# Attention and a gated mixture of experts on one core: a hand-searched order of TensorE's steps, and one weight load moved

## The chip, the cores and the metric

One core of one Trainium2 chip runs the whole kernel. The metric is the device time of one execution in microseconds (us), as the median of several runs. The core's engines work side by side, each through its own list of instructions: TensorE (PE) multiplies, its weight loads are shown apart as PEld; VectorE (DVE), ScalarE (ACT) and GpSimd (POOL) work elementwise; SyncE (SP) and GpSimd issue transfers. Semaphores make one engine wait for another.

## The reference

Sliding-window attention with four "sink" keys, for 4 batches, 8 heads, 768 positions and 64 elements a head, and then a mixture of 4 experts over the 3072 rows of 512 that come out of it:

```python
keep = is_sink | in_window                       # 4 sinks, a window of 128
scores = np.where(keep, q @ k.T / sqrt(D), -1e9)
a = exp(scores - max) / sum
x = (a @ v)  -> rows of H * D = 512

p = domain_probs / domain_probs.sum(-1)
for e in range(4):
    h = np.maximum(x @ w1[e], 0.0)               # 512 -> 1024
    out += p[:, e:e + 1] * (h @ w2[e])           # 1024 -> 512
```

## The kernel before

**Tiles and stages.** The work is cut by batch b (0 to 3) and by group g of 256 rows (three to a batch). Attention of a group runs by head pairs hp (four): `scores` (L676, products over 64 rows of the array, one half of it for each head of the pair), an exponential on ScalarE (L702), a mask on VectorE (L695), `values` (L743, and L736 for the sink part), a reciprocal and a scaling into `onat`. Sink scores are a product of their own (`sinks`, L637). In batch 0 q and k are transposed on TensorE (`transposes`, called "flip", L570) and the result rows too (`turn`, L801); from batch 1 on both go by transposing DMAs on SyncE's queue (L245 into `qkT`, L760 into `xT`).

The mixture takes a group's `xT` through expert e. A unit is one (b, g, e). A slow unit makes x @ w1 in four steps (L1051); a fast one uses a Strassen form of seven products P1 to P7 (L1138) on sums of tokens (`T`, VectorE) and of weights. The relu of batch 0 has no gate and may run on ScalarE or VectorE ("any"; L1064 and L1066 for slow units, L1157 and L1159 for fast ones). From batch 1 on it is fused with the gate on VectorE. The second product is `second` for batch 0 (L1388, 512 columns) and, from batch 1 on, `product`, a Strassen chain over all four experts (L1312, 256 columns) in the order P1, P2, P6, P5, P7, P3, P4. Six H buffers hold units between the two products. Six PSUM banks turn round among the attention's and the first products' tiles; two more hold the second products' sums.

**What sets the order.** There is no fixed list. The kernel, while it is being built, keeps a clock for each engine in the table `t` and emits instructions as it goes. The main loop (from L1446) runs until nothing is left. In each round it first issues transfers that are due from the list `loads` and transposes from `turns`, then work of the other engines up to TensorE's planned time (`flush`), token sums (`mix.tokens`) and sums for the Strassen forms (`mix.chore`, `next_form`). Then it lists TensorE's options, each with a planned ready time and a rank: attention steps (rank `DUE` when attention lags, else 3; a double score block 0.1 lower), `product` (`LOW_PRODUCT`, or -1 when VectorE is behind by more than `BEHIND` or `FULL` units live), steps of open units (2 + `STEP0` x position), opening a new unit (`OPEN`, less `EARLY` for a batch from 1 on), and `second` (1 or `LOW_SECOND`). It takes the one that is ready within 40 ns and has the lowest rank, or, where none is, the one ready first (L1512). About 700 such choices are made.

A score block is emitted for one head pair ("todo") or for two ("two"), where four PSUM banks are free at once.

**The other engines.** `later(engine, ready, slack, run)` puts an item on the list `pend`; `flush` (L145) serves the engine whose next start is earliest, and on it the item with the earliest ready + slack. An item marked "any" goes to ScalarE or VectorE, whichever is served first. The slacks are constants: `MASK_SLACK` for the masks of batches 1 to 3, `TOKEN` for token sums, `GATE` for gated relus, `FORM` for weight sums. `MARGIN` enters the due times of the sums of H.

**Loads.** `load_nat`, `load_v`, `load_w1` and `load_w2` issue on GpSimd's queue in the order of `loads`; for a batch's rows (q, k) a block is two transfers of 128 KB, v is one, a w1 or w2 is 1024 KB. When batch 0's attention is through (L1452), the loop adds w1 of expert 3, then for each row block tb of batch 1 its q and k, with v behind every second block; w2 of expert 3 stands ahead of block tb = `LAST`, 2. `turn_nat` plans when a block's transpose is through, with `LATE` added. `values_at` holds when a group's values are planned to be through.

**Batches.** The attention of batch b + 1 starts when batch b's is through and the mixture's work has passed a share `LEAD` of what lies ahead of it.

The choice itself is one line, L1512:

```python
        r, _, kind, step = min(opts, key=lambda o: (o[0] > now + 40, o[0] if o[0] > now + 40 else 0, o[1]))
```

Of the kernel before, what the change touches and what calls it, by code (L numbers as in the profile page):

```python
# [16 lines left out]
def kernel(  # L17
# [28 lines left out]
    NHP = H // 2  # L46
# [19 lines left out]
    LOW_PRODUCT = 2.147  # L66
    LOW_SECOND = 2.509
    HIGH_PRODUCT = -1
    EARLY = 0.1973
    MASK_SLACK = 200.0  # L70
    GATE = 2639.0
    GATE0 = 6000.0
    FORM = 1000.0
    TOKEN = 4559.0
    MARGIN = 2117.0
    HOLD = 0
    FULL = 8
    STEP0 = 0.2923
    READY = 40
    WIDE = 3  # L80
    OPEN = 2.551
    ONACT = 1
    ONE = 2
    PAIR = 0
    BEHIND = 2351.0
    CHORES = 3
    OWN = 2
    LAST = 2
    BIASED = 1
    FAST = tuple(START)  # L90
    BZ = 0
# [32 lines left out]
    def free_at(n=1):  # L124

        return sorted(ring)[n - 1]
# [276 lines left out]
    def next_form():  # L403

        if forming:
            return False
        x = next(((weight_form1, e) for e in FAST if form1_due(e)), None) or next(
            ((weight_form, e) for e in range(E) if form_due(e)), None)
        if x is None:
            return False  # L410

        def run(engine):
            forming.clear()
            x[0](x[1])
        forming.append(x)
        later("dve", t["pe"], FORM, run)
        return True

    forms_at = {}
# [237 lines left out]
    def scores(b, hp, g, more=False):  # L657
# [32 lines left out]
        if b == 0:  # L690
            part = join(2, masked)
        else:
            def mask_both(at):
                def run(engine):
                    nc.vector.tensor_mul(a, a, m[:, None, :].to_broadcast([P, 2, w]))  # L695
                    masked(dve(2 * w, rate=1.92))

                later("dve", at, MASK_SLACK, run)
            part = join(2, mask_both)
        for ph in range(2):  # L700
            def run(engine, ph=ph):
# [18 lines left out]
    def values(b, hp, g):  # L720
# [96 lines left out]
    class Attention:  # L817
# [15 lines left out]
        def more(self):  # L833
            return bool(self.todo or self.scored or self.valued)

        def two(self):
            return self.b >= PAIR and len(self.scored) <= 2 and len(self.todo) > 1 and self.todo[0][::3] == self.todo[1][::3] and self.todo[0][0] == "scores"

        def flip_ready(self):
            _, b, g, hp = self.flips[0]  # L840
# [3 lines left out]
        def options(self):  # L844

            if self.valued:
                yield turn_ready(*self.valued[0]), "turn"
            if self.scored and len(self.valued) < 3:
                yield values_ready(*self.scored[0]), "values"
            if self.todo:  # L850
                kind, b, x, y = self.todo[0]
                if kind == "scores":
                    if len(self.scored) < 4:
# [64 lines left out]
    class Mixture:  # L918
# [77 lines left out]
        def firsts(self):  # L996

            early = sum(map(len, self.early.values()))
            zero = sum(u["unit"][0] == 0 for u in self.open)
            n = len(self.open)  # L1000
            for i, u in enumerate(self.open):
                b, g, e = u["unit"]
                if u["fast"]:
                    for m in u["left"]:
                        yield max(u["at"].get(m, 1e12), free_at() if m == "P5" else 0.0), 2 + STEP0 * i, (u, m)
                else:
                    j = u["left"][0]
                    yield self.unit_ready(b, g, e, j < QF // 2), 2 + STEP0 * i, (u, j)
            if n < WIDE and early:
                at, g = self.next_early()  # L1010
                yield at, (OPEN if n else 2), ("early", g)
            if n < WIDE and self.units and early <= MIX and self.room() and not (early + zero and self.live >= NH - 1):
                yield self.unit_ready(*self.units[0], False), (OPEN if n else 2) - EARLY, ("unit",)

        def emit_first(self, what, ready):

# [57 lines left out]
            def run(engine):  # L1074
# [3 lines left out]
                at = dve(2 * G, fixed=152)  # L1078
                take(slot, at)
                part(at)  # L1080
            later("dve", end, GATE0, run)

        def tokens(self):

# [8 lines left out]
            if at > t["pe"]:  # L1093
                return
            at = t["pe"]
            x = xT[b, g]
# [9 lines left out]
            def run(engine):  # L1106
# [6 lines left out]
            later("dve", at, TOKEN, run)  # L1113

        def emit_fast(self, u, m, ready):
            b, g, e = u["unit"]
# [61 lines left out]
                later("dve", ready, slack, run)  # L1178

            if m == "P1":  # L1180
                u["last"] = join(2, lambda at: gated(H[:, 1, :, 1], tiles["X"], 1, at, GATE, slots["X"]))

                def seed(engine):
                    nc.scalar.copy(out=tiles["Y"], in_=y)  # L1184
# [15 lines left out]
            elif m == "P6":  # L1200
                u["both"](end)
            elif m == "P2":
                gated(H[:, 0, :, 1], y, 1, end, GATE, slots["Y"])
            elif m == "P7":
                def run(engine):
                    nc.vector.tensor_add(c5, c5, y)  # L1206
                    at["P4"] = dve(n)
                    gated(H[:, 1, :, 0], c5, 0, at["P4"], 100, then=u["last"])
                later("dve", end, 0, run)
            elif m == "P3":  # L1210
                gated(H[:, 0, :, 0], y, 0, end, GATE, slots["V"])
            else:
                u["last"](end)

        def chore(self):

            if self.chores >= CHORES:
                return False

            def go(fn, slack):  # L1220
# [43 lines left out]

        def until(self, b, g, e, m):
            n = self.products.index((b, g, m)) * E + self.order_of(b, g).index(e) - self.piece
            return max(0.0, n * QF * G / 2.4 - MARGIN)

        def operand(self, b, g, e, m):
            H = self.H[b, g, e]  # L1270
# [170 lines left out]
    def free_ring(x):  # L1441
        if ahead < 1 or turns and x[1] <= turns[0][0]:
            return True
        return t["hw"] < t["pe"] and not (turns and (turns[0][0], 0) in turned_at)

    while mix.more() or att.more():  # L1446
# [43 lines left out]
        due = ahead == 0 or att.steps * share <= (mix.done - upto) * att.total  # L1490
        opts = []
        if att.more():
            opts = [(max(r, now), (DUE if due else 3) - 0.1 * (step == "two"), "att", step) for r, step in att.options()]
        s2, p = mix.second_ready(), mix.product_ready()
        behind = max(t["dve"] - now, 0.0) + 500 * sum(x[2] == "dve" and x[0] < now + 300 for x in pend)
        opts.append((max(p, now), HIGH_PRODUCT if behind > BEHIND or mix.live >= FULL else LOW_PRODUCT, "product", None))
        opts += [(max(f, now), p, "first", x) for f, p, x in mix.firsts()]
        opts.append((max(s2, now), 1 if mix.since >= 1 else LOW_SECOND, "second", None))
# [6 lines left out]
        if soonest > 1e11:  # L1505
# [52 lines left out]
```

## Time and profile before

| | us |
|---|---|
| median of 3 runs | 363.13 |
| lowest, highest | 362.83, 363.67 |
| the profiled execution | 362.99 |
| its span | 361.2 |
| PE busy | 351.7 |
| DVE busy | 296.4 |
| ACT busy | 164.9 |
| POOL busy | 70.4 |

The span runs from the first instruction to the last; the profiled execution's time has 1.8 us more around it. Busy times are of one profiled execution. Matmuls overlap, so that a row's "mean ns of one" is a latency; the pace is read from the difference of two starts. A few matmul records are missing from a trace, so that a group of eight may be shown with seven. "Releaser" or "<-" names what ended an idle time. A line number is that of the kernel before.

### The profile page before, as it was taken

The page shows a single profiled execution, that of the slowest core. Times are in us where ns is not written, and L with a number is a line of the kernel's source. Part 1 is how long each engine was busy: PE and PEld are TensorE (multiplying, and loading weights), DVE is VectorE, ACT ScalarE, POOL GpSimd, SP SyncE. Part 2 cuts the span into 40 slices and gives each one's busy share as a digit, 9 for nine tenths or more (in the row PEclk, how much of TensorE's full clock was granted, in tenths as well). Part 3 has the DMA queues.
Part 4 walks back from the last instruction along what each step waited for, and adds up shares of the span by engine and source line. Part 5 has one row for each costly group of instructions (what it writes and reads, how often), then busy time and mean ns, then how long its engine had stood idle before and what let it go on. Part 6 is the DMA issues. An engine that isn't in the chain of part 4 may idle for free.

```text
span 361.2 us, 10566 instructions
## 1 busy us (share of the span) xinstructions
PE 351.7 (97%) x4410; PEld 296.2 (82%) x4423; DVE 296.4 (82%) x671; ACT 164.9 (46%) x419; POOL 70.4 (19%) x90
## 2 busy tenths in 40 slices
PE   8799999998999999999999999999999999999996
PEld 3485767756668868898899899899999999999985
DVE  4665999868868979789789989979999998987840
ACT  5764634557754463655464465546222223212110
POOL 8935016223500616101440000000000000000000
PEclk9999999999999999999999999999999999999999
DMA  9999999999943999917899131214113102000011
GB/s 172 182 186 201 210 209 177 149 126 184 149 92 97 146 175 152 135 49 74 128 155 174 16 104 31 55 50 62 37 25 89 31 22 85 16 29 33 0 61 58
DMA packets 117292, 37.25 MB, mean 103 GB/s; under 512 B 100613, under 2 KB 112741, under 8 KB 117245
## 3 DMA queue, kind: packets, MB, share of 16 engines
q0 software_dynamic: 77520, 17.31, 56.1%
q1 hardware_dynamic: 38668, 18.75, 26.0%
q8 instruction: 34, 0.56, 0.6%
q10 hardware_dynamic: 1056, 0.52, 0.5%
q14 instruction: 14, 0.11, 0.2%
HBM read 40.45 MB, written 6.34 MB: 130 GB/s over the span
## 4 chain that ended last, share of the span: by engine, by line
PE 72%; DMA 21%; POOL 4%; issue 1%; DVE 1%; ACT 0%; SPq 0%
PE acc L1312 31%; PE cps L1138 27%; DMA w<-in_moe_w_dram 11%; PE hps L1051 6%; DMA qkn<-in_k_dram 4%; DMA vx<-in_v_dram 3%; PE acc L1388 3%; DMA xT<-onat 2%; PE sps L676 2%; PE od L743 2%; POOL qkn L233 1%; POOL vx L298 1%; PE od L736 1%; POOL w L311 1%; POOL w L321 0%
## 5 line engine op out<-in xcount | busy, mean ns | idle before, releaser
L1138 PEld LDWEIGHTS <-w 128*128 128x128 bf16 x1184 | 73.3, 98 | 3.7 <-issue 1.5
L1312 PEld LDWEIGHTS <-H 128*128 128x128 bf16 x600 | 56.0, 98 | 6.2 <-issue 0.6
L702 ACT ACTIVATE aT<-sps 128x512 bf16<-128x512 f32 (+1 forms) x96 | 47.4, 573 | 18.5 <-PE sps L676 18.5
L1171 DVE SCALAR_TENSOR_TENSOR H<-cps,gates 128x512 bf16<-128x512 f32 x78 | 52.9, 682 | 1.3 <-PE cps L1138 0.2
L1138 PEld LDWEIGHTS <-vf 128*128 128x128 bf16 x768 | 47.3, 98 | 1.7 <-issue 0.4
L1312 PE MATMUL acc<-w,H 128*128 128x256 bf16 x360 | 47.7, 273 | 0.0
L1138 PE MATMUL cps<-T,w 128*128 128x128 bf16 x592 | 45.1, 219 | 0.1
L1138 PE MATMUL cps<-xT,w 128*128 128x128 bf16 x592 | 44.8, 219 | 0.0
L1388 PE MATMUL acc<-w,H 128*128 128x512 bf16 x179 | 43.4, 379 | 1.0 <-issue 0.5
L782 ACT ACTIVATE onat<-od,R 128x64 bf16<-128x64 f32 x144 | 32.9, 324 | 23.9 <-DVE R L770 23.9
L1051 PE MATMUL hps<-xT,w 128*128 128x256 bf16 x352 | 43.5, 273 | 0.1
L1184 ACT COPY cps<-cps 128x512 f32<-128x512 f32 x37 | 21.4, 579 | 38.4 <-PE cps L1138 32.8
L1138 PE MATMUL cps<-T,vf 128*128 128x128 bf16 x512 | 38.3, 219 | 0.1
L1051 PEld LDWEIGHTS <-w 128*128 128x128 bf16 x352 | 32.9, 98 | 5.6 <-issue 1.3
L1388 PEld LDWEIGHTS <-H 128*128 128x128 bf16 x192 | 17.8, 98 | 17.9 <-issue 0.3
L298 POOL DMA_DIRECT2D vx<-in_v_dram x24 | 21.4, 901 | 48.8 <-PE od L743 44.8
L1312 PEld LDWEIGHTS <-S 128*128 128x128 bf16 x288 | 27.2, 98 | 2.9 <-issue 0.2
L1191 DVE TENSOR_TENSOR cps<-H,cps 128x512 f32<-128x512 f32 x31 | 21.4, 692 | 8.4 <-PE cps L1138 5.5
L1360 ACT COPY osb<-acc 128x256 f32<-128x256 f32 x28 | 10.5, 373 | 38.3 <-PE acc L1312 38.3
L1312 PE MATMUL acc<-wf,H 128*128 128x256 bf16 x184 | 25.8, 273 | 0.0
L695 DVE TENSOR_TENSOR aT<-aT,mask 128x1024 bf16<-128x1024 bf16 (+1 forms) x36 | 22.8, 640 | 1.9 <-ACT aT L702 1.7
L1206 DVE TENSOR_TENSOR H<-H,cps 128x512 f32<-128x512 f32 x31 | 21.2, 683 | 3.8 <-PE cps L1138 3.7
(126 smaller groups left out, 543.9 us busy)
## 6 DMA issues: line engine op xcount, KB each, us to landing
w<-in_moe_w_dram POOLq DMA_DIRECT2D x7, 1024.0 KB, 16.2
out_dram<-osb SPq DMA_DIRECT2D x19, 256.0 KB
gates<-gate_rows SPq DMA_DIRECT2D x36, 128.0 KB
vx<-in_v_dram POOLq DMA_DIRECT2D x24, 128.0 KB, 6.9
qkn<-in_q_dram POOLq DMA_DIRECT2D x22, 128.0 KB, 6.8
qkn<-in_k_dram POOLq DMA_DIRECT2D x22, 128.0 KB, 7.2
w<-in_moe_w_dram POOLq DMA_DIRECT2D x2, 512.0 KB, 9.0
out_dram<-osl SPq DMA_DIRECT2D x4, 256.0 KB
```

What stands on the lines that cost most here:

```text
L298: nc.gpsimd.dma_start(out=vx[tb][:, :, 0:D], in_=v[b, :, tb * P:(tb + 1) * P, :].rearrange("h p d -> p h d"),)
L695: nc.vector.tensor_mul(a, a, m[:, None, :].to_broadcast([P, 2, w]))
L702: nc.scalar.activation(out=a[:, ph], in_=sps[ph][:, 0:w], func=AF.Exp, scale=scale)
L782: nc.scalar.mul(o[:, qi, hp, ph * D:(ph + 1) * D], od[:, qi, ph, 0:D], R[:, qi, ph])
L1051: nc.tensor.matmul(h[:, i].rearrange("p (q n) -> p q n", q=2), lhsT=w1_sb[e][:, db, fb * P:(fb + 1) * P], rhs=xT[b, g][:, :, db], start=(i ...
L1138: nc.tensor.matmul(y[:, f], lhsT=A[:, d, f * P:(f + 1) * P], rhs=T[:, d], start=(m in ("P1", "P5") and f == 0 and d == 0), stop=(d == 1), ...
L1171: nc.vector.scalar_tensor_tensor(out=dst, in0=src, scalar=0.0, in1=gate, op0=ALU.max, op1=ALU.mult)
L1184: nc.scalar.copy(out=tiles["Y"], in_=y)
L1191: nc.vector.tensor_add(tiles["V"], c5, tiles["X"])
L1206: nc.vector.tensor_add(c5, c5, y)
L1312: nc.tensor.matmul(x, lhsT=self.operand(b, g, e, m)[:, f], rhs=forms[e][m][:, f], start=(k == 0 and f == 0 and m in (("P1", "P5", "P2") if ...
L1388: nc.tensor.matmul(op, lhsT=H[:, fb // QF, fb % QF, s], rhs=w2_sb[e][:, fb, :], start=(fb == 0), stop=(fb == NFB - 1),)
```

## The change

The diff turns many of the planner's constants into tuples of four, read by `by(x)`: which entry counts depends on TensorE's planned time against `SPLIT` (60, 130 and 220 us). Most tuples repeat the old value four times. The entries that differ are in the diff below. In words:

- `OTHER` lists 30 of the main loop's choices by number, with 1, 2 or 3: at these the option with that place in the sorted list is taken, not the first (the last one, if the list is shorter).
- An "any" item is open to VectorE only if ScalarE's planned free time is not earlier than VectorE's plus `ANYLAG` (0, and 51.99 ns past 220 us).
- `LAST` 2 becomes 0: w2 of expert 3 is asked for right behind w1 of expert 3, ahead of all of batch 1's rows.
- `LATE` 500 becomes 618.6, `LEAD`'s first entry 1.026 becomes 1.027, and `DUE`, `MASK_SLACK`, `TOKEN`, `MARGIN`, `FULL` and `OPEN` change in some stretches.
- New switches stand at values that leave the old course: `FORCE`, `HELD`, `GPOS`, `LOADN`, `TOKENS0`.
- `values_at` is set at the fourth head pair of a group alone.

```diff
+    HELD = ("unit", "early")
     NGATE = 5
+    ANYLAG = (0.0, 0.0, 0.0, 51.99)
+    OTHER = {31: 1, 83: 1, 70: 1, 73: 1, 63: 3, 17: 1, 138: 1, 106: 1, 189: 1, 92: 1, 113: 2, 149: 2, 87: 1, 182: 2, 96: 3, 178: 2, 132: 1, 90: 1, 155: 1, 164: 1, 318: 1, 286: 2, 330: 1, 197: 1, 395: 1, 212: 2, 480: 1, 454: 2, 569: 2, 500: 2}
+    TOKENS0 = 0.0
+    SPLIT = (60000.0, 130000.0, 220000.0)
...
-    LEAD = (1.026, 0.9853)
-    DUE = 1.356
+    LEAD = (1.027, 0.9853)
+    DUE = (1.356, 1.646, 1.356, 1.356)
...
-    MASK_SLACK = 200.0
+    MASK_SLACK = (200.0, 984.1, 200.0, 200.0)
...
-    TOKEN = 4559.0
-    MARGIN = 2117.0
+    TOKEN = (4927.0, 4559.0, 4924.0, 4559.0)
+    MARGIN = (4621.0, 2117.0, 2117.0, 2117.0)
     HOLD = 0
-    FULL = 8
+    FULL = (8, 8, 8, 9)
...
-    OPEN = 2.551
+    OPEN = (2.551, 2.566, 2.551, 2.551)
...
-    LAST = 2
+    LAST = 0
+    GPOS = 0
+    LOADN = 0
...
+    def by(x):
+
+        return x[sum(t["pe"] > at for at in SPLIT)]
+
...
-    FLIP, LATE = 103.6, 500.0
+    FLIP, LATE = 103.6, 618.6
...
-                mine = [x for x in pend if x[2] == engine or x[2] == "any" and engine != "pool"]
+                mine = [
+                    x for x in pend if x[2] == engine or x[2] == "any" and (
+                        engine == "act" or engine == "dve" and max(t["act"], x[0]) >= max(t["dve"], x[0]) + by(ANYLAG))
+                ]
...
-        values_at[b, g] = done
+        if hp == NHP - 1:
+            values_at[b, g] = done
...
-    loads, turns = [(load_nat, 0, tb) for tb in (4, 5)] + [(load_v, 0, (4, 5))], []
+    loads, turns = [], []
     for e in (1, 2):
         loads += [(load_w1, e), (load_w2, e)]
+    loads[GPOS:GPOS] = [(load_nat, 0, tb) for tb in (4, 5)] + [(load_v, 0, (4, 5))]
...
-        if not att.more() and not loaded:
+        if not loaded and (len(loads) < LOADN if LOADN else not att.more()):
...
-        r, _, kind, step = min(opts, key=lambda o: (o[0] > now + 40, o[0] if o[0] > now + 40 else 0, o[1]))
-        assert r < 1e11
+        opts = [o for o in opts if o[0] < 1e11]
+        opts.sort(key=lambda o: (o[0] > now + 40, o[0] if o[0] > now + 40 else 0, o[1]))
+        r, _, kind, step = opts[min(OTHER.get(taken, 0), len(opts) - 1)]
+        taken += 1
```

More of the change, by code (lines that the diff above doesn't have):

```diff
@@ L415, in next_form @@
         forming.append(x)
-        later("dve", t["pe"], FORM, run)
+        later("dve", t["pe"], by(FORM), run)
         return True
@@ L696, in run @@
                     masked(dve(2 * w, rate=1.92))
-                later("dve", at, MASK_SLACK, run)
+                later("dve", at, by(MASK_SLACK), run)
             part = join(2, mask_both)
@@ L834, in more, with mate @@
             return bool(self.todo or self.scored or self.valued)
+        def mate(self):
+            return self.b >= by(PAIR) and len(self.todo) > 1 and self.todo[0][::3] == self.todo[1][::3] and self.todo[0][0] == "scores"
         def two(self):
-            return self.b >= PAIR and len(self.scored) <= 2 and len(self.todo) > 1 and self.todo[0][::3] == self.todo[1][::3] and self.todo[0][0] == "scores"
+            return len(self.scored) <= 2 and self.mate()
         def flip_ready(self):
@@ L852, in options @@
                 if kind == "scores":
-                    if len(self.scored) < 4:
+                    if len(self.scored) < 4 and not (by(FORCE) and self.mate()):
                         yield scores_ready(b, x, y), "todo"
@@ L1004, in firsts @@
                     for m in u["left"]:
[L1005 removed]
+                        yield max(u["at"].get(m, 1e12), free_at() if m == "P5" else 0.0), 2 + by(STEP0) * i, (u, m)
                 else:
                     j = u["left"][0]
[L1008 to L1009 removed]
+                    yield self.unit_ready(b, g, e, j < QF // 2), 2 + by(STEP0) * i, (u, j)
+            if n < by(WIDE) and early:
                 at, g = self.next_early()
[L1011 to L1013 removed]
+                yield at, (by(OPEN) if n else 2), ("early", g)
+            if n < by(WIDE) and self.units and early <= MIX and self.room() and not (early + zero and self.live >= NH - 1):
+                yield self.unit_ready(*self.units[0], False), (by(OPEN) if n else 2) - by(EARLY), ("unit",)
         def emit_first(self, what, ready):
@@ L1080, in run @@
                 part(at)
-            later("dve", end, GATE0, run)
+            later("dve", end, by(GATE0), run)
         def tokens(self):
@@ L1092, in tokens @@
             at = max(xT_at.get((b, hp, g), 1e12) for hp in range(NHP))
-            if at > t["pe"]:
+            if at > t["pe"] or b == 0 and t["pe"] < TOKENS0:
                 return
@@ L1112, in run @@
                     self.T_at[b, g] = done
-            later("dve", at, TOKEN, run)
+            later("dve", at, by(TOKEN), run)
         def emit_fast(self, u, m, ready):
@@ L1180, in emit_fast @@
             if m == "P1":
-                u["last"] = join(2, lambda at: gated(H[:, 1, :, 1], tiles["X"], 1, at, GATE, slots["X"]))
+                u["last"] = join(2, lambda at: gated(H[:, 1, :, 1], tiles["X"], 1, at, by(GATE), slots["X"]))
                 def seed(engine):
@@ L1202, in emit_fast @@
             elif m == "P2":
-                gated(H[:, 0, :, 1], y, 1, end, GATE, slots["Y"])
+                gated(H[:, 0, :, 1], y, 1, end, by(GATE), slots["Y"])
             elif m == "P7":
@@ L1210, in emit_fast @@
             elif m == "P3":
-                gated(H[:, 0, :, 0], y, 0, end, GATE, slots["V"])
+                gated(H[:, 0, :, 0], y, 0, end, by(GATE), slots["V"])
             else:
@@ L1215, in chore @@
         def chore(self):
-            if self.chores >= CHORES:
+            if self.chores >= by(CHORES):
                 return False
@@ L1266, in until @@
             n = self.products.index((b, g, m)) * E + self.order_of(b, g).index(e) - self.piece
-            return max(0.0, n * QF * G / 2.4 - MARGIN)
+            return max(0.0, n * QF * G / 2.4 - by(MARGIN))
         def operand(self, b, g, e, m):
@@ L1444, in free_ring @@
         return t["hw"] < t["pe"] and not (turns and (turns[0][0], 0) in turned_at)
+    taken = 0
     while mix.more() or att.more():
@@ L1492 @@
         if att.more():
-            opts = [(max(r, now), (DUE if due else 3) - 0.1 * (step == "two"), "att", step) for r, step in att.options()]
+            opts = [(max(r, now), (by(DUE) if due else 3) - 0.1 * (step == "two"), "att", step) for r, step in att.options()]
         s2, p = mix.second_ready(), mix.product_ready()
         behind = max(t["dve"] - now, 0.0) + 500 * sum(x[2] == "dve" and x[0] < now + 300 for x in pend)
-        opts.append((max(p, now), HIGH_PRODUCT if behind > BEHIND or mix.live >= FULL else LOW_PRODUCT, "product", None))
-        opts += [(max(f, now), p, "first", x) for f, p, x in mix.firsts()]
-        opts.append((max(s2, now), 1 if mix.since >= 1 else LOW_SECOND, "second", None))
+        opts.append((max(p, now), HIGH_PRODUCT if behind > by(BEHIND) or mix.live >= by(FULL) else by(LOW_PRODUCT), "product", None))
+        hold = by(FORCE) and due and att.two() and max(turned(att.b, att.todo[0][3], *(att.todo[i][2] for i in range(2)))) < now and free_at(4) > now
+        opts += [(max(f, now), p, "first", x) for f, p, x in mix.firsts() if not (hold and x[0] in HELD)]
+        opts.append((max(s2, now), 1 if mix.since >= 1 else by(LOW_SECOND), "second", None))
         soonest = min(o[0] for o in opts)
```

23 lines of the change are left out of this document (12 added, 11 removed).

## The prediction

> **What bounds the kernel now.** I read the page's busy times first, then the same by stretches, then what TensorE waited for. The page:
>
> ```profile
> span 361.2 us, 10566 instructions
> PE 351.7 (97%) x4410; PEld 296.2 (82%) x4423; DVE 296.4 (82%) x671; ACT 164.9 (46%) x419; POOL 70.4 (19%) x90
> ```
>
> By stretches (from and to in us, length, then busy us of PE, PEld, DVE, ACT and POOL with counts, granted clock, DMA share, GB/s):
>
> ```profile
> 0.00:10.00 10.00, 7.85 (x50) 3.82 (x50) 4.66 (x28) 5.70 (x13) 8.99 (x16) 1.00 1.36 170
> 10.00:20.00 10.00, 8.53 (x122) 5.67 (x121) 7.97 (x29) 8.06 (x18) 8.45 (x14) 1.00 1.68 189
> 40.00:50.00 10.00, 9.95 (x92) 7.44 (x91) 9.69 (x21) 4.27 (x10) 1.75 (x2) 1.00 1.18 210
> 80.00:90.00 10.00, 8.90 (x103) 6.08 (x103) 8.32 (x17) 7.08 (x24) 2.60 (x4) 1.00 1.38 181
> 90.00:100.00 10.00, 9.89 (x113) 6.08 (x114) 8.05 (x18) 7.70 (x26) 5.52 (x7) 1.00 2.20 152
> 120.00:130.00 10.00, 9.16 (x110) 7.01 (x109) 7.95 (x21) 4.58 (x10) 5.04 (x6) 1.00 2.38 153
> 190.00:200.00 10.00, 10.00 (x139) 9.10 (x137) 9.90 (x25) 4.42 (x14) 0.00 (x0) 1.00 1.08 150
> 350.00:361.20 11.20, 8.05 (x74) 6.96 (x72) 1.68 (x5) 1.12 (x3) 0.00 (x0) 1.00 0.13 47
> ```
>
> TensorE is the bound: 9.5 us of the span (361.2 - 351.7) are not busy. Of these 3.6 lie in the first 20 us (20 - 7.85 - 8.53), 3.2 in the tail after its last product (11.2 - 8.05), 1.10 in 80 to 90 and 0.84 in 120 to 130; 0.8 is left for all the rest, and at 190 a busy figure shows nothing to win. The granted clock is whole in each row. The waits of PE, in us in total, times, and the longest:
>
> ```profile
> PE acc L549 <- DVE lent L467: 1.4, 1, 1.4
> PE tr L570 <- DMA qkn<-in_k_dram: 1.1, 1, 1.1
> PE sinks L637 <- DMA qkT<-qkn: 0.8, 1, 0.8
> PE od L743 <- DVE aT L695: 0.7, 1, 0.7
> PE od L743 <- DMA vx<-in_v_dram: 0.6, 1, 0.6
> ```
>
> The first is the start, before any choice. The third and fourth are what a new order can still take away: 0.80 and 0.68 us, here in their places (start, length, instruction, the idle time before it):
>
> ```profile
> 84.32 0.29 PE L637 MATMUL sinks<-qkT,ksd 128*32 128x256 bf16 x4 [0.80 <-DMA qkT<-qkn]
> 129.43 0.35 PE L743 MATMUL od<-vx,aT 128*128 128x65 bf16 x6 [0.68 <-DVE aT L695]
> ```
>
> A busy PE hides one more cost, the crossing into and out of the score blocks, whose products use 64 rows of the array:
>
> ```profile
> 95.17 1.04 PE L1051 MATMUL hps<-xT,w 128*128 128x256 bf16 x8
> 96.14 0.39 PE L676 MATMUL sps<-qkT 64*128 64x128 bf16 x6
> 96.47 1.05 PE L1051 MATMUL hps<-xT,w 128*128 128x256 bf16 x8
> 97.35 1.89 PE L1388 MATMUL acc<-w,H 128*128 128x512 bf16 x7
> ...
> 99.17 0.62 PE L676 MATMUL sps<-qkT 64*128 64x128 bf16 x12
> 99.72 1.05 PE L1051 MATMUL hps<-xT,w 128*128 128x256 bf16 x8
> ```
>
> Read the starts. Eight L1051 products ahead of a score block take 0.97 us (96.14 - 95.17), the same eight ahead of another full-array product 0.88 (97.35 - 96.47): the entry costs 0.09. A lone score block (x6, one head pair) lasts 0.33 to the next start, a double (x12, two head pairs) 0.55. So two lone blocks cost 2 x (0.33 + 0.09) = 0.84, one double 0.55 + 0.09 = 0.64: each merge saves 0.20 us. The timeline has 14 lone blocks in batches 1 to 3, the first and the last being
>
> ```profile
> 73.74 0.34 PE L676 MATMUL sps<-qkT 64*128 64x256 bf16 x4
> ...
> 202.84 0.34 PE L676 MATMUL sps<-qkT 64*128 64x256 bf16 x4
> ```
>
> so at most 7 merges, 1.4 us, are left.
>
> The Trainium skill says that changing the tiling mode drains TensorE (TensorEngine Tiling (Array Packing), Tiling Modes, Key Properties), and TensorE: Matmul & The Clock Gate (Single matmul latency) puts a drain at about 175 ns. By these a merge would save an estimated 0.35 us, two drains, and the three merges of the sum below 1.05 in place of 0.6, for 361.4; the rows' 0.20 for a whole merge is the measurement and decides.
>
> **The change part by part.** Dead parts first. The new condition lets VectorE take an "any" item only if ScalarE's planned free time is at least VectorE's plus a lag. The lag is 0 until the planned TensorE time passes 220 us, and with 0 it says what the old rule says already: an engine is served when its next start is the earliest, ties going to ScalarE. The relus of the first batch, and the two copies of the "any" kind (L269), have ended by then:
>
> ```profile
> L1064 ACT ACTIVATE H<-hps x23: 597/597/636, 19.6 to 126.4; 128x512 bf16<-128x512 f32 x23
> L1157 ACT ACTIVATE H<-cps x13: 592/597/606, 54.8 to 85.2; 128x512 bf16<-128x512 f32 x13
> L269 ACT COPY xT<-tx x5: 367/372/392, 15.0 to 42.0; 128x256 bf16<-128x256 bf16 x5
> ```
>
> The last starts at 126.4, so the placing by backlog comes to 0. That holds unless other edits push a relu past 220 us, which none can. DUE and OPEN in their second phase move a rank between the same neighbours (1.646 stays between 1 and 2, 2.566 between 2.509 and 2.5846); FULL 9 guards a count that six H buffers cap; MARGIN 4621 applies below 60 us, where the sums it dates (chores of batch 1) do not exist yet; FORCE, HELD, LOADN, GPOS and TOKENS0 are off at their values; values_at is read only after the fourth head pair. All 0.
>
> LEAD[0] + 0.001 starts batch 2's attention a thousandth of the work ahead of it later, some 0.1 us of a third of the span, with products in its place: 0. LATE adds 0.12 us to when the planner believes a turned block of batches 1 to 3. It guards against waits like the 0.80 above, and its cost is a score block 0.12 later behind other products: 0 to +0.1, taken 0. TOKEN (4927 and 4924 for 4559) lets the token sums sit 0.37 us lower in VectorE's order, 0. MASK_SLACK (984 for 200) in 60 to 130 us lets VectorE put a mask (L695) up to 0.78 us later. Between a score block and its values lie products (L1051 and L1388 in the rows at 95 to 100), which cover that; the 0.68 above is such a cover run out, and a mask 0.78 later would add up to that much. I take 0 and keep +0.8 for the range.
>
> **The last w2** is asked for ahead of batch 1's first rows. Its neighbours on the POOL queue, and the chain of waits with what landed when (start, length):
>
> ```profile
> 27.83 0.75 POOL L311 DMA_DIRECT2D w<-in_moe_w_dram  x1
> ...
> 50.57 0.87 POOL L321 DMA_DIRECT2D w<-in_moe_w_dram  x1 [4.30 <-DMA w<-in_moe_w_dram]
> ```
> ```profile
> 27.83 27.32 DMA w<-in_moe_w_dram
> 56.34 14.92 DMA qkn<-in_k_dram
> 73.33 12.36 DMA vx<-in_v_dram
> ```
> ```profile
> 57.17 26.84 SPq L245 DMA_TRANSPOSE qkT<-qkn  x6
> ```
>
> The last w1 landed at 55.15 (27.83 + 27.32). Behind it stood two blocks of q and k and two of v, then the 1 MB of w2, then the other four blocks, of which the third's k landed at 71.26. One MB at the 210 GB/s of 40 to 50 us is 5.0 us. So the first two blocks, and batch 1's first scores at 73.74, come up to 5.0 us later: between 73.7, if the planner's wait and the transposing queue (26.84 us for six blocks) have slack, and 78.7. I take the middle. Blocks three to six have the same bytes ahead of them as before: 0, and so the sinks' 0.80 wait gets no worse by this. TensorE has products of the first batch in the meantime (9.95 busy in 40 to 50), and w2 itself lands some 3.7 us sooner (0.75 MB fewer ahead of it), which frees its products that much earlier: 0. If that cover is gone, up to +5.0.
>
> **The thirty listed steps.** Each takes the second, third or fourth of the ready list, so the same products in another order; the sum of PE work stays, and only merges and waits can change. Step 17 can be followed. The loop is the same up to it: values of the fourth head pair go ahead of the fourth pair's transposes.
>
> ```profile
> 12.10 0.49 PE L570 MATMUL tr<-ident,qkn 128*128 128x128 bf16 x3
> 13.73 0.90 PE L570 MATMUL tr<-ident,qkn 128*128 128x128 bf16 x13 [1.15 <-DMA qkn<-in_k_dram]
> ```
>
> PE's wait for the k rows falls after three transposes, inside the first head pair's, ahead of the swap: nothing is won there, at most 0.2 lost or gained in the order behind it. The other 29 act on a state that the earlier ones have changed. I bound them. Best: all 7 merges (1.4) and both waits (1.5) gone, -2.9. Worst: a wait like the 0.80 for each of a few steps, +2.4 for three. Counted along the old order, step 106 is the lone block at 73.74, so a product is to go ahead of it, after which a second head pair may have its banks and the two merge; steps 182 and 197 have lone blocks second on their lists, so they may part a pair as well as shift one. 20 of the 29 lie below step 200, which stood at 130 us: they reach the stretches with 1.10 and 0.84 idle. For the value I take half of the best, as the ends are far apart and the rows show both the idle time and the lone blocks to be there: three merges (0.6) and one of the two waits (0.7), -1.3.
>
> **The sum.** The profiled execution took 362.99 us, 361.2 of it span. 362.99 - 1.3 = 361.7; the median of three lies 0.14 above the profiled execution, so 361.8.
>
> **Rivals.** A, the order does not do what it is listed for: the steps exchange one lone block for another and the waits move, 363.1 (within 0.4). For it: PE's products are fixed and its row at 190 is full. Against: the two waits and 14 lone blocks.
>
> B, more: six merges and most of both waits, -2.5, so 362.99 - 2.5 + 0.14 = 360.6. Against: some head pairs are alone because a PSUM bank was not free.
>
> C, slower, by batch 1's rows: its first scores start past 76 us, the first batch's products run short before its first xT is turned, and PE waits once, between 95 and 130 us, for half of the 5.0: 363.13 + 2.5 = 365.6. It decides from the point where PE's wait for qkT or xT exceeds 1.3, the gain. For it: the w2 is ahead of what the next attention needs. Against: PE at 9.95 of 10 in 40 to 50 and 9.89 in 90 to 100, with products at hand on both sides.
>
> D, VectorE: masks or gated products late in 60 to 210 us, where DVE is at 9.90 of 10, so PE waits for aT or H two or three times at 0.7, less the merges: 363.13 + 1.6 - 0.6 = 364.1.
>
> **How the numbers follow.** Forecast 0.40, A 0.23, B 0.15, C 0.12, D 0.10. A measurement here tells 0.2%, 0.7 us, from no change. The forecast's own range is 361.0 to 362.6; most of it and all of B are faster by over 0.2%, a piece of A too: 0.54. The rest of A and the forecast's upper end are the same: 0.24. C and D: 0.22. The range reaches to B and through D, and cuts the upper half of C: 360.2 to 364.6.
>
> **What would show it.** Right: under 12 lone score blocks in batches 1 to 3, the idle before the first sinks or the value block under 0.3, PE's busy total lower by the merges, the tail still about 3.2. The w2 right: batch 1's first scores between 74 and 79, with no idle of PE before them. Wrong: 14 lone blocks and the same waits (A); an idle of PE over 1.3 us between 95 and 130 on qkT, xT or w (C); several on DVE (D). A relu of the first batch on another engine than before, at an unchanged place in the order, would show that the placing is not dead.

## The result, and the profile after

| | before | after |
|---|---|---|
| median, us (16 runs each) | 362.66 | 360.64 |
| ratio, 95% interval | | 0.9953 (0.9938 to 0.9968) |
| the profiled execution, us | 362.99 | 361.27 |
| its span, us | 361.2 | 359.6 |

The change makes the kernel 0.47% faster, about 1.7 us by the ratio, which is that of the means; the medians differ by 2.0. The page after, first two lines:

```profile
span 359.6 us, 10578 instructions
PE 351.3 (98%) x4424; PEld 296.5 (82%) x4424; DVE 297.1 (83%) x673; ACT 163.7 (46%) x417; POOL 70.4 (20%) x90
```

TensorE still bounds it, with 8.3 us of its span idle (359.6 - 351.3). What PE waited for (us in total, times, longest):

```profile
PE sps L691 <- DMA qkT<-qkn: 1.9, 1, 1.9
PE acc L564 <- DVE lent L482: 1.4, 1, 1.4
PE tr L585 <- DMA qkn<-in_k_dram: 1.2, 1, 1.2
PE od L758 <- DMA vx<-in_v_dram: 0.3, 2, 0.2
PE tx L817 <- DVE onat L788: 0.2, 1, 0.2
```

Against the same view of before, the waits of 0.8 (sinks for qkT) and 0.7 (values for a mask) are gone, and a new one of 1.9 has come, the largest in the kernel. The stretches show the same (from and to, length, busy us of PE, PEld, DVE, ACT and POOL, clock, DMA share, GB/s):

```profile
0.00:10.00 10.00, 8.26 (x52) 4.01 (x54) 4.86 (x28) 5.84 (x13) 8.99 (x16) 1.00 1.33 169
10.00:20.00 10.00, 8.44 (x122) 5.59 (x122) 7.92 (x29) 7.91 (x18) 8.47 (x14) 1.00 1.74 188
...
70.00:80.00 10.00, 8.09 (x83) 4.94 (x81) 7.44 (x18) 4.47 (x14) 1.75 (x2) 1.00 1.95 142
80.00:90.00 10.00, 10.00 (x113) 6.75 (x111) 7.84 (x18) 8.24 (x25) 0.00 (x0) 1.00 1.53 162
...
120.00:130.00 10.00, 10.00 (x111) 7.13 (x109) 8.21 (x19) 5.93 (x13) 1.57 (x2) 1.00 2.04 133
```

80 to 90 went from 8.90 to full and 120 to 130 from 9.16 to full, while 70 to 80 is down to 8.09, from 9.89 before:

```profile
70.00:80.00 10.00, 9.89 (x113) 6.65 (x113) 6.87 (x17) 6.07 (x16) 3.06 (x4) 1.00 2.37 127
```

From 80 us to the tail PE is now full in every stretch. The new wait, in the timeline of PE (start, length, instruction, idle before it), with the score blocks and the first sinks behind it:

```profile
71.85 1.89 PE L1407 MATMUL acc<-w,H 128*128 128x512 bf16 x8
75.65 0.34 PE L691 MATMUL sps<-qkT 64*128 64x256 bf16 x4 [1.91 <-DMA qkT<-qkn]
...
76.92 0.34 PE L691 MATMUL sps<-qkT 64*128 64x256 bf16 x4
...
84.02 0.29 PE L652 MATMUL sinks<-qkT,ksd 128*32 128x256 bf16 x4
84.25 0.62 PE L691 MATMUL sps<-qkT 64*128 64x128 bf16 x12
84.80 1.04 PE L1070 MATMUL hps<-xT,w 128*128 128x256 bf16 x8
```

75.65 is batch 1's first score block. The first sinks start at 84.02 without a wait, where before they started at 84.32 behind one of 0.80.

Score blocks: batches 1 to 3 had 14 lone ones and have 8, three merges. Batch 0 has one double parted, so 31 blocks stand for 33. From starts: for each pair of neighbouring products I took the time between their starts, less 1/2.4 ns a column and 2.5 ns, the pace at which most of them follow each other in these traces (eight products of 128 columns start 0.445 us after the eight before). What is over at the edges of the score blocks is 5.8 us in 61 crossings before and 5.1 us in 54 after, 0.095 each. Two more crossings of the changed kernel fall together with waits and are left out, so five are saved, 0.5 us. So the 1.6 us of span are roughly -1.5 (the two old waits), -0.5 (crossings), -0.3 (a shorter wait for v at 9 us) and +1.9 (the new wait), and about -1.2 in pieces under 0.3 us.

Neither the "any" rule nor the constants DUE, OPEN, FULL and MARGIN nor the place of values_at has a part in this. With the old ones put back in the changed kernel, the program that is built has the same instructions on all engines, in the same order. On ScalarE the relus of slow units fall from 23 to 22; as the program is the same without the new rule, the new order of steps does this.

### The profile page after: what moved, and what is told of

It is laid out like the page before. It is cut to its first block, busy times and chain, and to the rows that moved or that the text cites. A ratio compares the mean times of both kernels' runs of the same rounds, so it can differ in the third digit from the quotient of the medians.

```text
span 359.6 us, 10578 instructions
## 1 busy us (share of the span) xinstructions
PE 351.3 (98%) x4424; PEld 296.5 (82%) x4424; DVE 297.1 (83%) x673; ACT 163.7 (46%) x417; POOL 70.4 (20%) x90
## 4 chain that ended last, share of the span: by engine, by line
PE 78%; DMA 18%; POOL 3%; issue 0%; ACT 0%; DVE 0%; SPq 0%
PE acc L1331 31%; PE cps L1157 30%; DMA w<-in_moe_w_dram 8%; PE hps L1070 7%; DMA qkn<-in_k_dram 7%; PE acc L1407 5%; DMA qkT<-qkn 3%; PE sps L691 3%; PE od L758 2%; POOL qkn L248 1%; POOL vx L313 1%; PE od L751 1%; POOL w L326 0%; PE sinks L652 0%; POOL scratch L493 0%
## 5 line engine op out<-in xcount | busy, mean ns | idle before, releaser
L1407 PE MATMUL acc<-w,H 128*128 128x512 bf16 x192 | 45.2, 379 | 0.0
L248 POOL DMA_DIRECT2D qkn<-in_q_dram x22 | 19.7, 897 | 33.3 <-DMA qkT<-qkn 25.0
```

Of the source, the lines that this page charges most:

```text
L248: nc.gpsimd.dma_start(out=both[:, i], in_=src[b, :, tb * P:(tb + 1) * P, :].rearrange("h p d -> p h d"),)
L1407: nc.tensor.matmul(op, lhsT=H[:, fb // QF, fb % QF, s], rhs=w2_sb[e][:, fb, :], start=(fb == 0), stop=(fb == NFB - 1),)
```

## The experiments

Where a kernel's "order is written out", the list `OTHER` is replaced by a list of names of all 693 choices of the changed kernel (697 for the kernel before), and the loop takes the option with the next name:

```diff
-        r, _, kind, step = opts[min(OTHER.get(taken, 0), len(opts) - 1)]
+        chosen = next((o for o in opts if named(o) == PLAN[taken]), None)
+        if chosen is None:
+            assert flush(1e11, True)
+            continue
+        r, _, kind, step = chosen
```

In this list `s` is a score block, sinks or sink keys, `2` a double block, `S` a `second`, `v` values, `t` a turn, `f` a flip, `e1` the opening of a batch 0 unit of group 1, and 0033 step 3 of unit (0, 0, 3). All ratios are to the kernel before, with 95% intervals.

**The changed kernel again** (a0_after, no edit).

> The changed kernel once more, beside the others of this job. Expected: 0.995 of the time before (360.6 against 362.7 us), with PE idle for about 1.9 us on the transposed q and k ahead of batch 1's first scores.

Measured: 360.52 us, 0.9958 (0.9937 to 0.9979), with an idle of 2.0 us at the same place. The two measurements of the change agree.

**The w2 put back, the order kept** (a1_w2_back).

```diff
-    LAST = 0
+    LAST = 2
```

> The changed kernel with its order of choices written out and kept, so that PE, ACT, DVE and SP run the same instructions in the same order, and the last w2 asked for where it stood before (behind two row blocks of batch 1). Theory 1 (the 1.9 us idle ahead of batch 1's first scores comes from the w2 standing ahead of the rows): the idle falls under 0.3 us and the time by 1.6 to 1.9 us, to about 358.9. Theory 2 (the early w2 is what frees the second products of expert 3 and takes away the 0.68 us wait at 129 us, and the idle is due to the scores being put earlier): the idle stays over 1 us, and a new wait for w in 85 to 130 us brings the time to 360.6 or over.

Measured: 360.85 us, 0.9969 (0.995 to 0.9987): no gain. The idle ahead of the first scores is gone as theory 1 said, but the time is not. PE's timeline there:

```profile
81.56 0.34 PE L781 MATMUL od<-vx,aT 128*128 128x65 bf16 x6
83.41 0.29 PE L675 MATMUL sinks<-qkT,ksd 128*32 128x256 bf16 x4 [1.51 <-DMA qkT<-qkn]
```

PE reaches the first sinks some 2 us sooner and waits there for batch 1's fourth transposed block. The built program differs from the changed kernel's in the place of this one transfer alone. Theory 1 is right for the wait ahead of the first scores and wrong for the time; theory 2 has the time, but no wait for w came: nearly the same time is waited for at another place.

**The w2 further back, the order kept** (b1_w2_fourth, b2_w2_last: `LAST = 4` and `LAST = 6`).

> The changed kernel's order of choices written out and kept, with the last w2 behind four row blocks of batch 1 (where the changed kernel has none and the kernel before two). Theory 1 (each place of the w2 puts off the blocks behind it by its 5 us, so that with none ahead the first scores wait 1.9 us, with two the first sinks wait 1.5 us; with four ahead of it neither wait is left, and w2 still lands ahead of expert 3's second product at 86 us): PE's idle on qkT under 0.4 us, time 358.6 to 359.3. Theory 2 (the four blocks behind the fourth place or the w2 itself become the next late thing): a new wait of 1 us or more and 360.3 or over.

> The same with the last w2 behind all six row blocks of batch 1. Theory 1: the two waits stay away, but w2 lands close to the first second product of expert 3 (at 86 to 88 us), so that the time lies between 358.6 (no wait) and 361 (PE waits for w2 some 2 us). Theory 2: as with four ahead of it.

PE keeps its order in both; some items of VectorE and ScalarE, and with all six ahead also of SyncE, change places. With four blocks ahead of the w2: 360.51 us, 0.9956 (0.9944 to 0.9968), and again a wait ahead of the sinks, to nearly the same moment:

```profile
83.84 0.29 PE L675 MATMUL sinks<-qkT,ksd 128*32 128x256 bf16 x4 [1.96 <-DMA qkT<-qkn]
```

With all six ahead: 367.86 us, 1.0169 (1.0151 to 1.0187), the sinks without a wait, but w2 too late for expert 3's second product:

```profile
81.83 0.29 PE L675 MATMUL sinks<-qkT,ksd 128*32 128x256 bf16 x4
```
```profile
PE acc L1430 <- DMA w<-in_moe_w_dram: 5.6, 1, 5.6
```

When the fourth block is there can be read without a wait of PE too, from the completion events of its transposing DMA in the traces: at 81.51 us with the w2 ahead of all blocks (82.74 in a0_after), 83.28 with it behind two, 83.70 behind four, and 77.20 behind all six. Theory 1, by which each place of the w2 moves the blocks behind it by 5 us, is wrong for this block: with the w2 behind two or four blocks it comes later than with the w2 ahead of all, and only with the w2 behind all six is it several us sooner.

The transpose itself does not take the same time. From the end of its issue to its completion the fourth block's took 6.1 us with the w2 ahead of all, 7.1 behind two, 10.8 behind four and 7.3 behind six, with whatever it waited for the block before it on the queue. Three of batch 2 in the changed kernel, at 110 to 116 us, took 1.9 to 2.0 each, the first two while GpSimd's queue moved next to nothing. The run with four blocks ahead had the w2 itself on its way meanwhile (asked for at 60.23, landed at 81.04). I read this as loads and transposes slowing each other where they run side by side, so that what a block gains by an earlier load it can lose in its transpose; no run takes the two apart. The queue's issue rows fit: in the changed kernel four transposes take 12.91 us to issue, where three of batch 2 took 4.19 before (the 12.91 may hold waits for rows as well).

```profile
62.49 12.91 SPq L260 DMA_TRANSPOSE qkT<-qkn  x4
```
```profile
114.65 4.19 SPq L245 DMA_TRANSPOSE qkT<-qkn  x3
```

**Other work ahead of the sinks** (c1_sinks_later): the w2 behind two blocks, and in the list

```diff
-  S v s 2 0033 S 2 v e1
+  S v 0033 e1 s 2 S 2 v
```

> The changed kernel's order with the last w2 put back behind two row blocks (the run a1_w2_back, 360.85 us, where PE waited 1.5 us for batch 1's fourth transposed block ahead of its first sinks at 83.4 us), and three steps of the first batch's mixture (one second product, one first product, the opening of a unit, 3.5 us) put ahead of these sinks. Theory 1 (the fourth block of batch 1 is through at about 83 us in whatever order, since the transfers are the bound until then; the wait falls wherever PE comes to it first, and only other work put ahead of it removes it): no wait of PE for qkT over 0.3 us, time 1.3 to 1.6 us under a1, 359.2 to 359.6, and none of the longer executions that follow an idle of 2 us with a lower clock. Theory 2 (work put ahead only moves the sinks, and what waits for them waits in turn): a wait elsewhere in 84 to 130 us, 360.3 or over.

The expectation counts three steps; the edit moves two, a first product and the opening of a unit, 1.8 us (the second product stood ahead of the sinks already). Measured: 359.55 us, 0.991 (0.9895 to 0.9926). PE there:

```profile
81.74 0.34 PE L781 MATMUL od<-vx,aT 128*128 128x65 bf16 x6
81.92 1.91 PE L1093 MATMUL hps<-xT,w 128*128 128x256 bf16 x16
83.77 0.29 PE L675 MATMUL sinks<-qkT,ksd 128*32 128x256 bf16 x4
```

The sinks start at 83.77, close to where they did, and PE has done two first products more by then. The fourth block's transpose is complete at 83.47 (83.28 in a1), so the wait is gone, and 1.3 us with it by the medians of a1 and this run, 0.6% by their ratios. This is theory 1's sum (its "in whatever order" is too wide, as b2_w2_last shows), and with c3_both it is the fastest version, under the kernel before and under the changed one. It is the change's own order with the early w2 undone and two choices moved.

**The w2 alone** (a2_w2_alone): the kernel before with

```diff
-    LAST = 2
+    LAST = 0
```

> The kernel before with the w2's place alone moved; PE, ACT, DVE and SP keep their instructions and order, GpSimd's transfers alone differ. Theory 1: batch 1's first scores, at 73.7 us before, wait for q and k until about 75.7 as in the changed kernel, so PE idles 1.5 to 2 us more and the time rises by 1.0 to 2.0 us, to 363.7 to 364.7. Theory 2: no change or a gain (362.0 to 362.8).

Measured: 363.55 us, 1.0038 (1.0023 to 1.0053), slower as theory 1 said, but not by its wait. PE waits 0.8 us for qkT, ahead of the first scores now instead of the first sinks; the loss is at 128 us:

```profile
PE od L743 <- DVE aT L695: 2.1, 1, 2.1
```

VectorE's timeline just ahead of it:

```profile
125.21 1.28 DVE L1171 SCALAR_TENSOR_TENSOR H<-cps,gates 128x512 bf16<-128x512 f32 x2
129.91 0.29 DVE L1107 TENSOR_TENSOR T<-xT 128x256 bf16<-128x256 bf16 x1 [3.42 <-DMA xT<-onat]
130.12 0.55 DVE L695 TENSOR_TENSOR aT<-aT,mask 128x768 bf16<-128x768 bf16 x1
```

VectorE stands 3.42 us at a token sum whose xT is still being transposed, and the mask is queued behind it. PE, VectorE, ScalarE and SyncE have the same instructions in the same order as before. The kernel before has the same in small: its 0.68 us, which the view of waits puts down to the mask, has this ahead of it:

```profile
128.61 0.29 DVE L1107 TENSOR_TENSOR T<-xT 128x256 bf16<-128x256 bf16 x1 [2.05 <-DMA xT<-onat]
128.82 0.55 DVE L695 TENSOR_TENSOR aT<-aT,mask 128x768 bf16<-128x768 bf16 x1
```

Why the transpose ends later here is not shown. It is issued at nearly the same time, first in the kernel before and then in this one:

```profile
120.10 1.75 SPq L760 DMA_TRANSPOSE xT<-onat  x1
```
```profile
119.81 2.71 SPq L760 DMA_TRANSPOSE xT<-onat  x1
```

It is complete at 128.59 before and at 129.88 here, though the w2 had landed long ago in both (at 66.8 and 60.4 us). So the place of the w2 can act on it only in a roundabout way, or the 1.3 us is one execution's, as each kernel has one trace; the 0.38% itself stands over twelve executions.

**The masks ahead of the token sums** (d1_mask_first): a2's kernel with its order written out, and

```diff
-                    xT_at[b, x, g] = turned_out
+                    xT_at[b, x, g] = turned_out + (3000.0 if (b, g) == (1, 2) else 0.0)
```

by which the planner puts the four sums behind three masks of batch 2; on no other engine does an instruction move.

> The kernel before with the w2 put ahead (a2_w2_alone, 363.55 us, where PE waited 2.1 us at 128 us for a mask), its order of choices kept, and on VectorE three masks of batch 2 put ahead of four token sums that wait for a transposed xT; no other engine's instructions change. Theory 1 (the mask is late since it is queued behind the token sums, and they behind a transposing DMA that the late row loads slow): the wait falls to under 0.3 us and the time by 1.8 to 2.1, to 361.4 to 361.8, under the kernel before, which has 0.7 of the same wait. Theory 2 (the mask waits for its own scores or for an exponential): no change, 363.3 to 363.8.

Measured: 362.33 us, 1.0000 (0.9991 to 1.0009), 0.38% or 1.4 us under a2 by the ratios. The wait at 128 us is gone; VectorE runs the masks as their exponentials come, and the sums later:

```profile
128.12 0.56 DVE L733 TENSOR_TENSOR aT<-aT,mask 128x768 bf16<-128x768 bf16 x1 [0.70 <-ACT aT L740]
128.89 0.56 DVE L733 TENSOR_TENSOR aT<-aT,mask 128x768 bf16<-128x768 bf16 x1 [0.21 <-ACT aT L740]
```

So the mask was late because it was queued behind the token sums: this half of theory 1 holds. That late row loads slow the transpose is not shown, and in this trace the transpose was also complete sooner, at 128.45. The gain is less than the 1.8 to 2.1 expected: the view of waits has 1.2 us at the first scores, for 0.8 in a2, and one of 0.9 for an exponential, which lies at 8.9 us, far ahead of the edit.

**LATE with the w2** (b4_late_alone): a2's kernel and

```diff
-    FLIP, LATE = 103.6, 500.0
+    FLIP, LATE = 103.6, 618.6
```

> The kernel before with the w2 put ahead and LATE at 618.6, all else as before (363.55 us without the LATE, in the first set). 32 score blocks, of the same sizes as in the changed kernel without its steps (361.83). Theory 1 (LATE, by its 0.12 us, makes the planner put other products ahead of batch 1's and 2's scores, and so brings the 1.7 us between those two): 361.5 to 362.2. Theory 2 (the slacks of masks and token sums bring it): 363.2 to 364.

Measured: 361.92 us, 0.9991 (0.9973 to 1.0008), 0.47% under a2. Theory 1: beside the early w2, LATE brings nearly all of what lies between a2 and the changed kernel without its listed steps (a3_no_steps, 0.9985), and the slacks, TOKEN and LEAD, which a3 has besides, bring nothing that can be told. The order built with it has neither of a2's two waits, the 0.8 at the first scores and the 2.1 at 128 us. LATE without the early w2 was not run.

**The steps undone** (a3_no_steps): `OTHER = {}` in the changed kernel.

> The changed kernel with the list of thirty steps empty; all the rest stays, the w2's early place too. The program has 32 score blocks for 31 of the changed one and 33 of before. Theory 1 (the steps bring the merges and take away the waits at 84 and 129 us, and the w2 costs 1.9): the time is over the kernel before, 363 to 364.5. Theory 2 (the steps shift blocks about, the gain is from the w2 and the slacks): 360.5 to 361.5.

Measured: 361.83 us, 0.9985 (0.9975 to 0.9996): between the two theories. By the ratios of this kernel and the changed one the steps are worth 0.32% of the 0.47%, about 1.2 us. Without them batches 1 to 3 have 13 lone blocks for 8 (and one block of three head pairs, so 24 blocks for 22), and PE has no wait for qkT, 0.4 us of the one for a mask, and 0.4 for a sum of H:

```profile
PE od L758 <- DVE aT L710: 0.4, 1, 0.4
PE cps L1157 <- DVE H L1225: 0.4, 1, 0.4
```

**A merge's price** (b3_split): at 13 places of the changed kernel's list

```diff
-  2 X
+  s X s
```

> The changed kernel's order with 13 double score blocks of batches 1 to 3 parted: the product behind each is put between its two head pairs; 44 score blocks for 31. Theory 1 (a merge is worth 0.20 us, as read from starts at 95 to 100 us): 2.6 us more than the changed kernel, 363.1. Theory 2 (a drain on each side, 0.35 us a merge): 4.6 us more, 365.1. Theory 3 (the crossing is hidden by other waits): under 1 us more.

Measured: 363.50 us, 1.0043 (1.0025 to 1.0061), 3.0 us over a0_after. The starts have 80 crossings for 54 and 2.44 us more at them: 0.094 a crossing, 0.19 a merge; the rest of the 3.0 us is not placed. Theory 1; the 0.35 of theory 2 is out.

**Step 17 undone** (c2_no_step17), alone and on top of c1 (c3_both): `v t f` at choices 17 to 19 is `f t v` again.

> The changed kernel's order written out, with step 17 alone undone (the fourth transposes of group 1 ahead of the fourth values again). The program has 30 score blocks for 31 (two of batch 0 are one again) and one idle product fewer. Theory 1 (step 17 wins nothing, as PE's wait for k rows lies ahead of it, and its part costs one parted block and the idle product): 0.1 to 0.3 us less than the changed kernel, 360.2 to 360.4. Theory 2 (it fills the wait): 0.2 to 0.4 us more, 360.8 to 361.

> c1_sinks_later with step 17 undone as well: by theory 1 of both 359.0 to 359.4, the fastest of all.

Measured: 360.44 us, 0.9937 (0.9923 to 0.9952), and 359.52 us, 0.9914 (0.9896 to 0.9931). Neither differs from its partner (the changed kernel, 0.9953, and c1, 0.991) beyond the intervals. No gain of the step is seen; a gain or a cost of 0.1 to 0.4 us is too small to tell here, so neither theory is settled.

## Why the prediction was right, and where its steps were not

The time, 360.64, lies in the range, and the change is -1.7 us by the ratio (0.47%) beside a forecast of -1.3. The forecast's own range, 361.0 to 362.6, misses it, and the number is rival B's 360.6. Part of that is the starting point: the forecast set out from 363.13, the median of three, where sixteen executions of the kernel before have 362.66; the measured ratio on 363.13 gives 361.4, inside. Of B's mechanism one half came, both old waits gone; of merges there were the forecast's three, not six; and a wait of 1.9 us came that neither had. So the time near B's is luck. The terms one by one:

**Dead parts: right.** The placing of relus, DUE, OPEN, FULL and MARGIN change no instruction. LEAD, TOKEN and MASK_SLACK, taken as 0, bring nothing that can be told where no steps are listed (b4_late_alone and a3_no_steps, 0.9991 and 0.9985); no run prices them one by one.

**The thirty steps: right in sum, not in kind.** Predicted -1.3, from three merges and one of two waits; a3_no_steps puts the steps at about -1.2. Lone blocks in batches 1 to 3 fell from 14 to 8 by the whole change, three merges, at 0.19 us a merge (b3_split) for 0.20 predicted. By the steps alone they fell from 13 to 8, which with step 17's parted block leaves four crossings fewer, 0.4 us. Of the two old waits, the one at the sinks is gone without the steps too, and 0.3 us of the one for the mask. What the steps took of waits is 0.4 us for the mask and 0.4 for a sum of H, and the 1.9 us ahead of the first scores came with them. By these rows the steps would cost 0.7 us. The profiled spans fall by 0.5 instead (360.1 to 359.6), and the times by 1.2, so that 1.2 to 1.9 us lie in pieces too small to name, and stay open. That the sum agrees with the forecast is luck to that extent.

**Step 17: not contradicted**: no gain was seen. Its parted block and its extra filler product (one more product of zeros, which only fills PE's time) were not foreseen.

**LATE: mis-sized.** Taken as 0 to +0.1, as a delay of 0.12 us. With the w2 early it is worth -0.47% (b4_late_alone against a2_w2_alone): the small shift of a planned time changes which order is built, and the one built has neither of a2's waits of 0.8 and 2.1 us.

**The last w2: mis-sized, and wrong in its reason.** Its delay was taken as covered by the first batch's products. The size of the delay was right: the second block's transpose is complete at 75.51 with the w2 ahead and at 71.04 with it put back (a1), 4.5 us for up to 5.0. First scores did come later (75.65, inside the 73.7 to 78.7), but with 1.9 us of PE idle ahead of them, so the cover had run out; "with no idle of PE before them" was wrong. "Blocks three to six have the same bytes ahead of them as before: 0" was mis-sized: the fourth block is there sooner with the w2 ahead of all, at 81.51 or 82.74 (a0) for 83.28 (a1), and in a2 the sinks' old wait is gone. In the old order the w2 alone costs 0.38%. The wait that grew there is PE's at 128 us, for a mask behind the xT transpose (a2, d1), a chain that the prediction did not have; how the w2 makes that transpose later is not shown. In the new order it costs and wins nothing that can be told (a1).

**Rival C** had the resource right (PE waiting for qkT since the w2 is ahead) but the place wrong: it put the wait at 95 to 130 us, as products running short; it came at 73.7 us, ahead of the first scores. Its 1.9 us is over the 1.3 at which C was to decide, and the kernel is faster all the same, so that threshold was wrong too. Rival D's rule, that a late mask stalls PE, came true in a2 and not in the changed kernel.

**The 0.68 us wait** was read as a mask that came late by VectorE's load. It was a mask behind a token sum that waited for a DMA. The row "od <- DVE aT" names the last releaser; VectorE's own idle time, 2.05 us on xT, was one view further.

In short: the sum came out because the steps' total agrees, by pieces that were not predicted, and because two terms taken as 0 nearly cancel in the one order in which they were measured, the w2 at about +0.4% and then LATE at about -0.5%; the two together are 0.9991 (b4_late_alone), no difference from before that can be told.

## What to carry to other kernels

Where TensorE is full, a new order is worth the mode crossings it merges, here 0.19 us a pair, and the waits it fills; count both in the trace. Moving one load may only move a wait: here three places of the w2 gave the same time, and the wait turned up at another first use. Find in the trace when the data is there, and put other products ahead of its first use. When a view names an in-order engine as the releaser, look at what that engine waited for just before.

## What the runs showed of the hardware

A single idle of 2.0 us on TensorE was once followed by a lower clock. In a0_after's profiled execution (362.69 us, span 361.0) the stretches behind the idle of 2.02 us, which ended at 75.6, show a granted clock (the third number from the end) of about a half for some 4 us:

```profile
74.00:76.00 2.00, 0.39 (x6) 0.26 (x7) 2.00 (x4) 0.03 (x1) 0.00 (x0) 1.00 1.71 143
76.00:78.00 2.00, 2.00 (x22) 1.51 (x21) 1.36 (x3) 1.26 (x3) 0.00 (x0) 0.54 2.00 155
78.00:80.00 2.00, 2.00 (x22) 1.47 (x23) 0.87 (x3) 1.53 (x5) 0.00 (x0) 0.60 1.65 157
80.00:82.00 2.00, 2.00 (x26) 1.51 (x25) 1.84 (x4) 1.93 (x8) 0.00 (x0) 1.00 1.46 221
```

In the changed kernel's first profile an idle of 1.91 us at the same place left the clock at 1.00 in the stretches of 70 to 90 us. The Trainium skill (TensorE: Matmul & The Clock Gate, HAM oscillation — how this bites in real kernels) gives gaps over about 3.4 us as the ones that throttle; here a gap of 2.02 us was followed by it once. Of the 25 executions of the changed kernel (after and a0_after) five have a mean clock of 0.994 or 0.995 and took some 2 us more, 362.7 to 363.1. Not all of this need be the wait: a clock of 0.995 also occurs in a1_w2_back, where the wait is 1.5 us (two of 12 executions, 363.3 and 364.1), and in the kernel before, where the wait is 0.8 and those executions lie among the others. In b2_w2_last the idle of 5.6 us was followed by a clock of 0.50:

```profile
92.80:95.00 2.20, 1.93 (x5) 0.76 (x6) 0.00 (x0) 0.00 (x0) 0.19 (x1) 0.50 1.30 72
95.00:97.00 2.00, 2.00 (x16) 1.16 (x15) 0.55 (x1) 0.00 (x0) 1.74 (x3) 0.50 0.03 2
```
